# Linear attention with MoE: the store of a finished x behind the spread of quotients, a fifth buffer of numerators, the reciprocal behind the last decoding step

## The chip, the cores and the metric

One NeuronCore of a Trainium2 chip runs the kernel. The metric is the device time of one execution in microseconds (us). The kernel before takes 1066.59 us, the median of three runs (1066.25 to 1066.69).

## The reference

Attention without a softmax over the keys, for 8 batches, 8 heads, 576 positions and 64 values a head, and then a two-layer MLP on its result:

```python
def phi(x):
    proj = np.einsum('bhsd,df->bhsf', x, w_phi)
    proj = proj - np.max(np.abs(proj), axis=-1, keepdims=True)
    return np.concatenate([np.exp(proj), np.exp(-proj)], axis=-1)
q_p, k_p = (phi(q), phi(k))
kv = np.einsum('bhsf,bhsd->bhfd', k_p, v)
z = np.sum(k_p, axis=2)
num = np.einsum('bhsf,bhfd->bhsd', q_p, kv)
den = np.einsum('bhsf,bhf->bhs', q_p, z)[..., None] + 1e-06
x = num / den
...
h = x @ w_in
g = h - np.tanh(h)
return (g @ w_out).astype(np.float32)
```

The numerator `num` is divided by the denominator `den`; the quotient x is what the MLP reads.

## The kernel before

The program has two stages. In the first, attention goes through 32 units, a unit being two heads of one batch. In the second, the MLP multiplies the finished x by the weights. Both weight matrices arrive as 64-bit numbers and are decoded to float32 on the way, one tile of 128 x 512 in each period of the first stage.

`period(i)` (L644 to L703) is one pass of the first stage, for i from 3 to 31; `ramp` stands before it and `drain` behind it. The order of the work is written out by hand: the program sets a manual schedule, and each engine runs its instructions in the order in which the calls stand in `period`. A period works on six units at once, `a, c, p, r, q, o`, which are the units i, i-1, i-2, i-3, i-4 and i-5. What a unit goes through, with the names that the steps below use:

- **Unit a, the projection and its centring.** PE projects q and k (`project`, L327) into three places in PSUM: `pj`, `pa` and `pt`. DVE takes the largest absolute value of each (`m`, L345) and subtracts it (`t`, L346), in the order pj, pt, pa (`centre`). `pa` shares its PSUM bank with the numerators `po`: one buffer for both.
- **Unit c.** Its exponentials are taken, and `kv` multiplies keys by values (`pc`, L393, which reads the tile `v`).
- **Unit p.** `num` computes the numerators on PE (`po`, L442), and `num_copy` (L464 to L469) copies them by ACT into `d`, a tile of 128 x 576. The tile has four buffers: one in the pool `p1` for each fourth unit (tag `d0`), three in the pool `tail` for the rest and for the last three units (tag `d`).
- **Unit r.** `denom` computes the denominators on PE, `denom_copy` (L473) puts them into `dd`, and `den_recip_load` (L478) has SP's queue lay them out over 128 partitions as `dn`. At the end of the period `den_recip` (L483) takes the reciprocals `rn` on DVE, and `den_store` (L488) writes them to `rr` in DRAM.
- **Unit q.** `den_spread` (L493) reads `rr` back in two DMAs and spreads it as `rb`, a single buffer.
- **Unit o.** `den_mul` (L496) multiplies `d` by `rb` on POOL, and `x_store` (L499) writes the product, the finished x, to `xs` in DRAM.

A weight tile is decoded in five steps (`dec_0` on ACT, L279; `dec_1`, `dec_2` and `dec_3` on DVE, L283, L284, L287 and L291). They use the PSUM bank `pt` as scratch, behind its centring. On DVE the end of a period reads: L283, L284, L287, the reciprocal L483, then L291.

DMAs start from two queues. SP's queue takes, in the order of a period, `xs`, `dn`, `rb` twice, `v` (`load_v`, L307), up to two stores of prepared weights (`wd`, L112) and `rr`. ACT's queue takes the raw weights (L267, L272) and `qk` (L303). SP runs its DMA instructions one after the other, and an instruction that waits holds those behind it.

In `drain`, behind the last period, the last five units are finished while the second stage starts. The copies of units 30 and 31 stand there (L469), and the stores of units 27 and 28 (L499).

Of the kernel before, what the change touches and what calls it, by code (L numbers as in the profile page):

```python
# [9 lines left out]
F32 = mybir.dt.float32  # L10
# [10 lines left out]
P = 128  # L21
# [12 lines left out]
def tile_linear_attention_moe(  # L34
# [11 lines left out]
    B, H, S, D = dims  # L46
# [180 lines left out]
    with ExitStack() as c1:  # L227
        c0 = ExitStack()
        pq = c0.enter_context(tc.tile_pool(name="pq", bufs=2, side="right"))
        c1.enter_context(tc.tile_pool(name="padp", bufs=1)).tile([P, 8], F32, name="padp")  # L230
        p1 = c1.enter_context(tc.tile_pool(name="p1", bufs=1))
# [54 lines left out]
        def dec_2(u):  # L286
            nc.vector.scalar_tensor_tensor(u.a, u.lo, 29, u.a, ALU.logical_shift_right, ALU.bitwise_or)  # L287

        def dec_3(u):
            w = wpool.tile([P, DM], F32, tag="w", name=f"w{u.nm}")  # L290
            nc.vector.scalar_tensor_tensor(  # L291
                w.bitcast(U32), u.hi, 0x80000000, u.a, ALU.bitwise_and, ALU.bitwise_or
            )
            u.d[u.f] = w
# [5 lines left out]
        def load(u, queue=nc.sync):  # L300
            u.qk = pq.tile([P, PC], F32, tag="qk", name=f"qk{u.i}")
            for o, w in ((0, PC),) if u.i else ((5 * P, PC), (0, 5 * P)):
                queue.dma_start(u.qk[:, o:w], qkT[u.i][:, o:w])  # L303
# [6 lines left out]
        def project(u, parts):  # L310
            for part in parts:
                if u.t is None:
                    u.t = [pq.tile([P, 2, 5, F], F32, tag="t0", name=f"t{u.i}_0"), None]
                    u.m = [p2.tile([P, 2, 5], F32, tag="m0", name=f"m{u.i}_0"), p2.tile([P, 2, 4], F32, tag="m1", name=f"m{u.i}_1")]
                if part == "j":
                    u.pj = ps_pj.tile([P, 2, 512], F32, tag="pj", name=f"pj{u.i}")
                    bank, tiles = u.pj, range(4)
                elif part == "t":
                    u.pt = ps_t.tile([P, 2, 512], F32, tag="pt", name=f"pt{u.i}")
                    bank, tiles = u.pt, range(4, 5)  # L320
                else:
                    u.pa = ps_d.tile([P, 2, 512], F32, tag="po", name=f"pa{u.i}")
                    bank, tiles = u.pa, range(5, 9)
                for k, a in enumerate(tiles):
                    for e in range(2):
                        hs = slice(e * D, (e + 1) * D)
                        nc.tensor.matmul(  # L327
                            bank[:, e, k * F : (k + 1) * F], u.qk[hs, a * P : (a + 1) * P], wph[hs, :], start=True, stop=True
                        )
# [10 lines left out]
        def centre(u, parts, h=None):  # L340
            for part in parts:
                x, m, t = part_of(u, part)
                if h is not None:
                    x, m, t = x[:, :, h], m[:, :, h], t[:, :, h]
                nc.vector.tensor_reduce(m, x, AX.X, ALU.max, apply_absolute_value=True)  # L345
                nc.vector.tensor_tensor(t, x, m.unsqueeze(3).broadcast_to(list(t.shape)), ALU.subtract)  # L346
# [54 lines left out]
        def kadd(u):  # L401
            x = p2.tile([P, 2, 2, F], F32, tag="ss", name=f"ss{u.i}")
            nc.gpsimd.tensor_tensor(x, u.kp[:, :, 1], u.kp[:, :, 2], ALU.add)
            nc.gpsimd.tensor_tensor(x, x, u.kp[:, :, 3], ALU.add)
            nc.gpsimd.tensor_tensor(x, x, u.kp[:, :, 4], ALU.add)
            nc.gpsimd.tensor_tensor(x, x, u.kp[:, :, 0], ALU.add)
            u.ss = x
# [14 lines left out]
        def ksum_turn(u):  # L422
            nc.tensor.transpose(u.pu[:, 0:F], u.kst, ident)
# [38 lines left out]
                        )  # L462

        def num_copy(u):  # L464
            if u.i % 4 or u.i >= NU - 3:
                u.d = tail.tile([P, S], F32, tag="d", name=f"d{u.i}", bufs=3)
            else:
                u.d = p1.tile([P, S], F32, tag="d0", name=f"d{u.i}")
            nc.scalar.copy(u.d.rearrange("p (c n) -> p c n", c=2), u.po[:, :, 0:CH])  # L469

        def denom_copy(u):
# [18 lines left out]
        def den_spread(u):  # L490
            u.rb = tail.tile([P, S], F32, tag="rb", name=f"rb{u.i}", bufs=1)
            for e in range(2):
                nc.sync.dma_start(u.rb[e * D : (e + 1) * D, :], u.rr[e : e + 1, :].broadcast_to([D, S]))  # L493

        def den_mul(u, pin=lambda ins: ins):
            pin(nc.gpsimd.tensor_tensor(u.d, u.d, u.rb, ALU.mult))  # L496

        def x_store(u):
            nc.sync.dma_start(xs[u.b // 2][u.hp, :, (u.b % 2) * S : (u.b % 2 + 1) * S], u.d)  # L499

        units = []
        for i in range(B * NHP):
            u = Unit()
# [3 lines left out]
        NU = len(units)  # L507
# [9 lines left out]
        def unit(i):  # L517
            return units[i] if 0 <= i < NU else None

        def bank():  # L520
            return ps_c.tile([P, 512], F32, tag="pu", name="pu")
# [40 lines left out]
        for n, k in enumerate(order[:EARLY_K]):  # L562
            p = Prep(k, nc.gpsimd, early_tile, early_stage).steps()
            o = 5 + 7 * (n // 2) + 3 * (n % 2)
# [24 lines left out]
        def aside_at(i, late):  # L589
            for f in aside[i][late]:  # L590
                f()
# [57 lines left out]
        def period(i):  # L649
            a, c, p, r, q, o = (unit(i - n) for n in range(6))  # L650
            w = dec[i - 3]
            if i < NU - 1:
                aside_at(i, False)
            if o:
                den_mul(o)
                x_store(o)
            project(a, "jat")
            centre(a, "jt")
            kadd(c)
            aside_at(i, True)  # L660
            dec.append(dec_load(i - 2, nc.scalar))
            if i + 2 < NU:
                load(units[i + 2], nc.scalar)
            pu = bank()
            if r:
                denom(r, pu)
            ksum(p, pu)
            if r:
                denom_copy(r)
                den_recip_load(r)  # L670
            if q:
                den_spread(q)
            if i > 3:
                load_v(a)
            aside_at(i, 2)
            aside_at(i, 3)
            ksum_copy(p)
            kv_turn(p)
            kv_turn_copy(p)
            dec_0(w, a.pt)  # L680
            q_turn(c)
            ksum_turn(p)
            q_turn_rest(c, pu)
            q_exp(c)
            q_exp_rest(c)
            ksum_turn_copy(p)
            centre(a, "a")
            k_exp(a, 0)
            kv(c)
            kv_copy(c)  # L690
            k_exp(a, 1, (0,))
            dec_1(w)
            dec_2(w)
            if r:
                den_recip(r)
                den_store(r)
            dec_3(w)
            if i == NU - 1:
                x0_split(0)
            num(p)  # L700
            num_copy(p)
            if i < NU - 1:
                k_exp(a, 1, (1,))  # L703
# [98 lines left out]
        for i in range(3, NU):  # L802
            period(i)
# [487 lines left out]
```

## Time and profile before

| what | value |
|---|---|
| time, median of three runs | 1066.59 us |
| time of the profiled execution | 1067.74 us |
| its span | 1065.7 us |
| PE busy | 1052.3 us (99%) |
| DVE busy | 877.4 us (82%) |
| ACT busy | 781.4 us (73%) |
| POOL busy | 274.6 us (26%), nearly all of it in the first 310 us |
| PE on the chain that ended last | 89% |

The span lies between the first and the last instruction of the profiled execution. What its own time has beyond the span, 2.0 us, lies around it. A busy share is a mean over both stages; the first stage, about the first 315 us, has its own balance of engines and nearly all of the DMA traffic that the change touches. The granted clock of TensorE is the full one (1.00) in every stretch that was read.

### The profile page before, as it was taken

Reading aid. Unit: us, or ns where it says so; the run is one execution under the profiler, and the core shown is the slowest. Engines: PE = TensorE matmul, PEld = TensorE weight load, DVE = VectorE, ACT = ScalarE, POOL = GpSimd, SP = SyncE. Lnnn points to the kernel's source line nnn. Section 1 sums busy time; section 2 is a strip of 40 time slices with the busy share of each in tenths; the row PEclk is TensorE's granted clock in tenths of the full one; section 3 lists DMA queues with packets and bytes.
Section 4 is the critical chain, followed back from the end, with each engine's and each line's share of the span. In section 5 each row is a group of like instructions: output and inputs, shape, how many; then the busy total and the mean of one; then the engine's idle time right before and its main releaser. Section 6 shows DMA issues by size and latency. Waiting matters only on the chain.

```text
span 1065.7 us, 18843 instructions
## 1 busy us (share of the span) xinstructions
PE 1052.3 (99%) x7244; PEld 885.8 (83%) x7244; DVE 877.4 (82%) x1110; ACT 781.4 (73%) x1252; POOL 274.6 (26%) x235
## 2 busy tenths in 40 slices
PE   8999999999999999999999999999999999999998
PEld 6667666776658989999999999999999999999997
DVE  7999889999988988877887688877878778876776
ACT  5888788887888777776777676766677766776665
POOL 4798889898990000000000000000000000000000
PEclk9999999999999999999999999999999999999999
DMA  5688898999856463355444533355334543353311
GB/s 179 190 234 265 259 279 266 279 271 257 248 176 227 155 205 132 122 199 181 130 137 164 184 120 119 109 182 194 116 112 135 196 138 132 120 178 109 120 50 59
DMA packets 75593, 184.56 MB, mean 173 GB/s; under 512 B 15728, under 2 KB 30448, under 8 KB 75504
## 3 DMA queue, kind: packets, MB, share of 16 engines
q1 hardware_dynamic: 61104, 150.99, 43.0%
q10 hardware_dynamic: 14400, 32.38, 10.9%
q8 instruction: 57, 0.93, 0.4%
q14 instruction: 32, 0.26, 0.1%
HBM read 149.49 MB, written 33.70 MB: 172 GB/s over the span
## 4 chain that ended last, share of the span: by engine, by line
PE 89%; DVE 4%; POOL 2%; DMA 2%; ACT 1%; issue 1%; SPq 0%; DVEq 0%; POOLq 0%; ACTq 0%
PE A L142 18%; PE B L142 13%; PE po L946 12%; PE po L947 12%; PE po L952 12%; PE pc L393 6%; PE po L442 5%; PE pj L327 3%; PE pu L456 3%; PE pa L327 2%; PE ptt L357 2%; DMA dn<-dd 1%; PE pc L431 1%; PE pt L327 1%; POOL d L496 1%
## 5 line engine op out<-in xcount | busy, mean ns | idle before, releaser
L142 PE MATMUL A<-xo,wr 128*128 128x384 f32 x1152 | 231.9, 337 | 2.2 <-ACT u L870 2.2
L142 PEld LDWEIGHTS A<-xo,wr 128*128 128x128 f32 x1152 | 204.7, 188 | 14.6 <-ACT u L870 3.3
L142 PE MATMUL B<-xo,wr 128*128 128x384 f32 x864 | 174.1, 337 | 2.7 <-DVE xo L553 1.3
L870 ACT COPY u<-A 128x384 f32<-128x384 f32 x144 | 68.9, 479 | 140.3 <-PE A L142 139.9
L142 PEld LDWEIGHTS B<-xo,wr 128*128 128x128 f32 x864 | 152.4, 188 | 7.5 <-DVE xo L553 1.6
L946 PE MATMUL po<-who,ghx 128*128 128x512 f32 x288 | 112.3, 390 | 0.0
L946 PE MATMUL po<-who,ghy 128*128 128x512 f32 x288 | 112.3, 390 | 0.0
L947 PE MATMUL po<-wlo,ghy 128*128 128x512 f32 x288 | 112.1, 389 | 0.0
L947 PE MATMUL po<-wlo,ghx 128*128 128x512 f32 x288 | 112.1, 389 | 0.0
L496 POOL TENSOR_TENSOR d<-d,rb 128x576 f32<-128x576 f32 x32 | 46.6, 1457 | 203.3 <-DMA rb<-rr 171.4
L909 DVE SCALAR_TENSOR_TENSOR s2y<-s2y,thy 128x768 f32<-128x768 f32 x48 | 46.1, 960 | 57.1 <-ACT thy L900 57.1
L382 ACT ACTIVATE kp<-t 64x256 f32<-64x256 f32 (+1 forms) x126 | 88.4, 726 | 2.5 <-DVE t L346 1.0
L952 PE MATMUL po<-who,glx 128*128 128x512 f32 x288 | 80.9, 389 | 0.0
L894 ACT ACTIVATE yx<-hx 128x768 f32<-128x768 f32 (+1 forms) x49 | 41.0, 836 | 53.3 <-DVE hx L877 53.3
L952 PE MATMUL po<-who,gly 128*128 128x512 f32 x282 | 79.2, 389 | 0.0
L393 PE MATMUL pc<-kp,v 128*64 128x256 f32 x640 | 76.1, 384 | 0.0
L442 PE MATMUL po<-qe,kv 128*64 128x288 f32 x512 | 68.1, 408 | 0.0
L952 PEld LDWEIGHTS po<-who,glx 128*128 128x128 f32 x288 | 54.0, 188 | 11.2
L906 DVE SCALAR_TENSOR_TENSOR s2x<-s2x,yx 128x768 f32<-128x768 f32 (+1 forms) x49 | 46.2, 942 | 20.6 <-ACT s2x L895 19.2
L393 PEld LDWEIGHTS pc<-kp,v 128*64 128x64 f32 x640 | 43.1, 136 | 23.8 <-issue 4.5
L952 PEld LDWEIGHTS po<-who,gly 128*128 128x128 f32 x282 | 52.8, 188 | 11.1 <-DVE gly L924 0.2
L946 PEld LDWEIGHTS po<-who,ghx 128*128 128x128 f32 x288 | 54.1, 188 | 8.1 <-DVE hy L881 0.4
(174 smaller groups left out, 2262.0 us busy)
## 6 DMA issues: line engine op xcount, KB each, us to landing
wr<-wd SPq DMA_DIRECT2D x92, 512.0 KB, 3.5
wr<-wd SPq DMA_DIRECT2D x46, 768.0 KB, 4.3
qk<-in_qkT ACTq DMA_DIRECT2D x27, 576.0 KB, 6.9
v<-in_v SPq DMA_DIRECT2D x32, 320.0 KB, 5.3
rb<-rr SPq DMA_DIRECT2D x64, 144.0 KB, 4.7
xs<-d SPq DMA_DIRECT2D x32, 288.0 KB, 5.9
out<-o SPq DMA_DIRECT2D x35, 256.0 KB, 2.1
rawo<-in_moe_w_out ACTq DMA_DIRECT2D x16, 512.0 KB, 5.8
```

The costliest lines, as they stand in the source:

```text
L142: nc.tensor.matmul(bank[:, 0:HT], w[:, a, n, cs], x[:, b, c, :], start=start and i == 0, stop=i == 5, skip_group_check=not start,)
L327: nc.tensor.matmul(bank[:, e, k * F : (k + 1) * F], u.qk[hs, a * P : (a + 1) * P], wph[hs, :], start=True, stop=True)
L382: nc.scalar.activation(u.kp[h, :, j, s, :], u.t[r][h, :, x, :], AF.Exp, scale=1.0 - 2.0 * s)
L393: nc.tensor.matmul(u.pc[e * D : (e + 1) * D, 0 : 2 * F], u.v[:, j, e, :], u.kp[:, e, j, :, :], start=(j == first), stop=(j == last))
L442: nc.tensor.matmul(u.po[e * D : (e + 1) * D, c, 0:CH], u.kv[:, s, e * D : (e + 1) * D], u.qe[:, e, s, c * CH : (c + 1) * CH], start=(s == ...
L496: pin(nc.gpsimd.tensor_tensor(u.d, u.d, u.rb, ALU.mult))
L870: nc.scalar.copy(t, A[q][:, 0:HT])
L906: nc.vector.scalar_tensor_tensor(z.s[:, s], z.s[:, s], GC, z.y[:, s], ALU.add, ALU.mult)
L909: nc.vector.scalar_tensor_tensor(z.s[:, s], z.s[:, s], GK, z.th[:, s], ALU.mult, ALU.mult)
L946: nc.tensor.matmul(po, z.gh[:, ts], wh, start=first, stop=False)
L947: nc.tensor.matmul(po, z.gh[:, ts], wl, start=False, stop=False)
L952: nc.tensor.matmul(po, z.gl[:, ts], wh, start=False, stop=last)
```

## The change

It makes three edits, all in the first stage.

```diff
         def num_copy(u):
-            if u.i % 4 or u.i >= NU - 3:
+            if u.i >= NU - 3 or u.i % 5 > 1:
                 u.d = tail.tile([P, S], F32, tag="d", name=f"d{u.i}", bufs=3)
+            elif u.i % 5 or u.i >= NU - 6:
+                u.d = p1.tile([P, S], F32, tag="d0", name=f"d{u.i}")
             else:
-                u.d = p1.tile([P, S], F32, tag="d0", name=f"d{u.i}")
+                u.d = pq.tile([P, S], F32, tag="d1", name=f"d{u.i}", bufs=1)
...
             if o:
                 den_mul(o)
-                x_store(o)
...
             if q:
                 den_spread(q)
+            if o:
+                x_store(o)
...
             dec_1(w)
             dec_2(w)
+            dec_3(w)
             if r:
                 den_recip(r)
                 den_store(r)
-            dec_3(w)
```

`pq` is the pool on the right side of SBUF that holds `qk`, `v` and `t`. With the fifth buffer, unit u shares its buffer with unit u+5 where it was u+4, except for the last units: unit 30 takes the buffer of unit 27 (before: of unit 26), and unit 31 that of unit 28 (before: of unit 27).

The first place is SP's queue in period 14 (`rr10` is the reciprocals of unit 10 on their way to DRAM, `d9` the product of unit 9). Before:

```order
L488 DMA rr10_1828<-rn10_1826 128x9 [waits DMAHW7_49,DVE_49]
L499 DMA xs1_89<-d9_1575 128x576 [waits DMAHW0_49,Pool_49]
L478 DMA dn11_1903<-dd11_1901 128x1x9 [waits DMAHW3_49,Activation_49]
L493 DMA rb10_1905<-rr10_1828 64x576 [waits DMAHW7_49,DMAHW4_49,DMAHW2_49]
L493 DMA rb10_1905<-rr10_1828 64x576 [waits DMAHW5_49]
L307 DMA v14_1908<-in_v5 128x640 [waits DMAHW6_49,PE_49]
L112 DMA wd3_0_101<-wr3_0_1446 128x512
```

After:

```order
L490 DMA rr10_1830<-rn10_1828 128x9 [waits DMAHW7_49,DVE_49]
L480 DMA dn11_1902<-dd11_1900 128x1x9 [waits DMAHW2_49,Activation_49]
L495 DMA rb10_1904<-rr10_1830 64x576 [waits DMAHW3_49,DMAHW7_49,DMAHW1_49,Pool_49]
L495 DMA rb10_1904<-rr10_1830 64x576 [waits DMAHW4_49]
L501 DMA xs1_89<-d9_1575 128x576 [waits DMAHW5_49]
L307 DMA v14_1908<-in_v5 128x640 [waits DMAHW6_49,PE_49]
L112 DMA wd3_0_101<-wr3_0_1446 128x512
```

The store `xs` moved behind the load `dn` and both spreads `rb`, and the wait for POOL's product went from the store to the first spread.

The second place is DVE at the end of period 17. Before:

```order
L283 TENSOR_SCALAR pt17_2271<-pt17_2271 128x512 [waits Activation_49]
L284 TENSOR_SCALAR pt17_2271<-pt17_2271 128x512 [waits DVE_49]
L287 SCALAR_TENSOR_TENSOR pt17_2271<-rawo4_2151,pt17_2271 128x512 [waits DMAHW5_49,DVE_49]
L483 RECIPROCAL rn14_2360<-dn14_2304 128x9 [waits DMAHW3_49,DMAHW0_49]
L291 SCALAR_TENSOR_TENSOR wo4_2364<-rawo4_2151,pt17_2271 128x512 [waits DVE_49]
L345 TENSOR_REDUCE m18_0_2384<-pj18_2386 128x2x4 [waits PE_49]
```

After:

```order
L283 TENSOR_SCALAR pt17_2270<-pt17_2270 128x512 [waits Activation_49]
L284 TENSOR_SCALAR pt17_2270<-pt17_2270 128x512 [waits DVE_49]
L287 SCALAR_TENSOR_TENSOR pt17_2270<-rawo4_2150,pt17_2270 128x512 [waits DMAHW4_49,DVE_49]
L291 SCALAR_TENSOR_TENSOR wo4_2360<-rawo4_2150,pt17_2270 128x512 [waits DVE_49]
L485 RECIPROCAL rn14_2362<-dn14_2303 128x9 [waits DMAHW7_49,DMAHW3_49]
L345 TENSOR_REDUCE m18_0_2383<-pj18_2385 128x2x4 [waits PE_49]
```

The reciprocal and its wait for the DMA moved behind the last decoding step; behind it comes, as before that step did, the first centring of the next unit.

The third place is ACT in `drain`, where unit 30's numerators are copied. Before:

```order
L427 COPY ks30_4307<-pu_4237 128x128 [waits PE_49,Activation_49]
L377 ACTIVATE qe31_4304<-pu_4237 128x2x64 x2
L399 COPY kvt31_4322<-pc31_4311 128x256 [waits PE_49,Activation_49]
L469 COPY d30_4349<-po30_4332 128x576 [waits DMAHW1_49,PE_49,Pool_49]
L279 ACTIVATE pt_4351<-rawo14_4266 128x512 [waits DMAHW3_49,DVE_49]
```

After:

```order
L427 COPY ks30_4307<-pu_4237 128x128 [waits PE_49,Activation_49]
L377 ACTIVATE qe31_4304<-pu_4237 128x2x64 x2
L399 COPY kvt31_4322<-pc31_4311 128x256 [waits PE_49,Activation_49]
L471 COPY d30_4349<-po30_4332 128x576 [waits DMAHW0_49,PE_49,Pool_49]
L279 ACTIVATE pt_4351<-rawo14_4266 128x512 [waits DMAHW3_49,DVE_49]
```

The order stayed, but the copy now waits on another DMA's semaphore: the store of unit 27 in place of that of unit 26.

## Rows read from the trace of the kernel before

**Rows 1.** Windows: a stretch, its length, busy us of each engine, PEclk, DMA share, GB/s

```profile
30.00:300.00 270.00, 268.44 (x3086) 185.42 (x3086) 244.96 (x342) 220.17 (x429) 238.72 (x201) 1.00 0.86 252
...
98.00:134.00 36.00, 34.82 (x408) 24.12 (x405) 30.95 (x46) 27.96 (x54) 30.43 (x27) 1.00 0.89 254
```

**Rows 2.** Timeline, a plain period, DVE: start us, us, instruction, [idle before <-releaser]

```profile
163.92 1.23 DVE L346 TENSOR_TENSOR t<-pa,m 128x1024 f32<-128x1024 f32 x1
...
166.52 0.70 DVE L287 SCALAR_TENSOR_TENSOR pt<-rawo,pt 128x512 uint32<-128x512 uint32 x1
167.13 0.21 DVE L483 RECIPROCAL rn<-dn 128x9 f32<-128x9 f32 x1
167.25 0.69 DVE L291 SCALAR_TENSOR_TENSOR wo<-rawo,pt 128x512 uint32<-128x512 uint32 x1
168.50 1.23 DVE L345 TENSOR_REDUCE m<-pj 128x8 f32<-128x1024 f32 x1 [0.56 <-PE pj L327]
```

**Rows 3.** Timeline, the same plain period, PE

```profile
165.25 2.12 PE L442 MATMUL po<-qe,kv 128*64 128x288 f32 x16
167.29 1.16 PE L327 MATMUL pj<-wph,qk 64*128 64x128 f32 x16
```

**Rows 4.** Timeline, the period with the longest wait, DVE

```profile
115.00 1.23 DVE L346 TENSOR_TENSOR t<-pa,m 128x1024 f32<-128x1024 f32 x1
...
120.20 0.22 DVE L483 RECIPROCAL rn<-dn 128x9 f32<-128x9 f32 x1 [1.91 <-DMA dn<-dd]
...
120.88 1.22 DVE L345 TENSOR_REDUCE m<-pj 128x8 f32<-128x1024 f32 x1
```

**Rows 5.** Timeline, that period and the next, PE

```profile
118.37 1.16 PE L327 MATMUL pj<-wph,qk 64*128 64x128 f32 x16
...
121.02 0.49 PE L327 MATMUL pt<-wph,qk 64*128 64x128 f32 x4 [0.58 <-DVE wi L291]
...
124.82 2.38 PE L393 MATMUL pc<-kp,v 128*64 128x256 f32 x20
```

**Rows 6.** Timeline, DVE, the other reciprocals that waited over 0.60 us

```profile
99.58 0.22 DVE L483 RECIPROCAL rn<-dn 128x9 f32<-128x9 f32 x1 [0.66 <-DMA dn<-dd]
109.48 0.22 DVE L483 RECIPROCAL rn<-dn 128x9 f32<-128x9 f32 x1 [1.10 <-DMA v<-in_v]
148.99 0.22 DVE L483 RECIPROCAL rn<-dn 128x9 f32<-128x9 f32 x1 [0.98 <-DMA dn<-dd]
262.41 0.22 DVE L483 RECIPROCAL rn<-dn 128x9 f32<-128x9 f32 x1 [0.88 <-DMA dn<-dd]
```

**Rows 7.** Timeline, SP's queue in the period with the longest wait

```profile
111.95 0.32 SPq L499 DMA_DIRECT2D xs<-d  x1
112.72 0.59 SPq L478 DMA_DIRECT2D dn<-dd  x1
...
114.78 0.59 SPq L307 DMA_DIRECT2D v<-in_v  x1
```

**Rows 8.** DMA issues, whole run: count, KB each, median us from issue to landing

```profile
v<-in_v SPq DMA_DIRECT2D x32, 320.0 KB, 5.3
...
xs<-d SPq DMA_DIRECT2D x32, 288.0 KB, 5.9
...
rr<-rn SPq DMA_DIRECT2D x32, 4.5 KB, 3.3
```

**Rows 9.** Timeline of `drain`: SP, DVE, ACT; last, the view of tile xs

```profile
303.04 0.32 SPq L499 DMA_DIRECT2D xs<-d  x1
303.46 0.59 SPq L478 DMA_DIRECT2D dn<-dd  x1
...
305.92 0.21 DVE L483 RECIPROCAL rn<-dn 128x9 f32<-128x9 f32 x1 [0.40 <-DMA dn<-dd]
...
306.95 0.64 ACT L469 COPY d<-po 128x576 f32<-128x576 f32 x1 [1.01 <-issue]
...
DMA to landing us min/median/max: 2.1/5.9/8.0
```

## The prediction

> **What bounds the kernel now.** I read the view by stretches first. In the first stage PE is busy 268.4 of 270 us, DVE 245.0 and POOL 238.7 [rows 1], at the full granted clock, and DMA moves 252 GB/s with its engines at a share of 0.86. So PE has next to no time to give, and what can be won is a wait that stretches a period. The change touches no PE work and nothing in the second stage except by starting it earlier.
>
> The timeline of one plain period shows what sets its length. DVE ends the centring of `pa` at 165.15 (163.92 + 1.23) [rows 2]. This frees the bank in which PE then writes `po`, from 165.25, and behind it PE projects `pj` from 167.29 to 168.45 [rows 3]. DVE begins the next unit's centring at 168.50, after an idle time of 0.56 us that `pj` ended [rows 2]. From the end of `t<-pa` to `m<-pj` it is 3.35 us, and the rest of the loop is DVE's own centring up to the next `t<-pa`. So the loop runs through DVE (centring) and PE (`po`, `pj`), and the decoding and the reciprocal lie beside the PE part, with 0.56 us to spare. The reader is to see that a reciprocal that waits up to 0.56 us costs nothing, and that each tenth beyond it lengthens the period.
>
> The view of DVE's reciprocals gives what goes beyond. The longest wait is 1.91 us, for `dn` [rows 4]; four more are over 0.60 us: 0.66, 1.10, 0.98 and 0.88 [rows 6]. The second of these is put down to another transfer, `v`; since the reciprocal reads `dn` alone, I take that label for a landing at the same time. The shorter ones cost next to nothing. Less 0.56 each, the five are 1.35, 0.10, 0.54, 0.42 and 0.32, together 2.73 us. The longest can be checked: `t<-pa` ends at 116.23 and `m<-pj` starts at 120.88 [rows 4], 4.65 us in place of 3.35, so 1.30 and not 1.35. With 0.05 us off each, **the late reciprocals cost 2.5 us** of the profiled execution. In the worst period the late decoding step also held PE's projection into `pt` for 0.58 us [rows 5]; that lies inside the 1.30.
>
> **The change part by part.** No instruction is added or removed; all three edits move or rename.
>
> *The last decoding step ahead of the reciprocal.* In a plain period DVE ends L287 at 167.22, and the reciprocal takes 0.21 us [rows 2]. If only the reciprocal is left to come, it may start as late as 168.45 - 0.21 = 168.24 before the next centring is late, so its wait may last 1.0 us in place of 0.56. The decoding step fills it, and frees `pt` for PE. Alone this would bring the waits of 0.66, 0.88 and 0.98 to nothing, leave about 0.1 of the one of 1.10 and about 0.85 of the longest (`pj` ends at 119.53 [rows 5], the reciprocal at 120.42 [rows 4]). It gains 2.5 - 0.9 = 1.6 us. In a plain period it starts `rr` some 0.6 us later. The spread behind `rr` waits for a landing that takes 3.3 us [rows 8], and may be 0.6 us later at the worst; it gains more than that by the next edit, since the store no longer runs ahead of it.
>
> *The store behind the spread.* Before, 288 KB of `xs` [rows 8] went to SP's queue 0.77 us ahead of `dn` [rows 7], so `dn` had to be moved behind them. `dn` took from 112.72 [rows 7] to the reciprocal at 120.20 [rows 4], 7.5 us for 4.5 KB; that is a queue, not a transfer. How much earlier it lands no row shows. The lower bound is nothing, if other transfers hold it. The upper bound is the 5.9 us from a store's issue to its landing [rows 8]. At the 254 GB/s of that stretch [rows 1], 288 KB take 1.16 us, an estimate; I take this one, as it is what the queue does with these bytes. It is more than the 0.85 us that the first edit leaves, so the worst period is repaired too. A gain below nothing has no place: behind the change fewer bytes stand ahead of `dn`, and POOL's product no longer does.
>
> What now stands behind the spread pays: the store starts about 2.5 us later, and `v` by one SP issue, 0.32 us [rows 7], and what lies around it, say 0.4. `v` issued at 114.78 [rows 7] lands after 5.3 us [rows 8] at 120.1, and the multiplication that reads it starts at 124.82 [rows 5], so 4 us of cover stand behind a loss of 0.4. The spread now waits itself for POOL's product; that product is done before the store's issue at 111.95 [rows 7], while the spread comes after `dn`. It costs nothing; were POOL 1 us later, `v` and the weight stores would be.
>
> The Trainium skill, in "DMA: Bandwidth & Descriptors", section "Queues, rings and completion order", speaks against taking the whole 1.16 us: the count that reports a DMA is a strongly ordered write, which lands only after every earlier write of that engine, across its queues. By that, `dn` still waits for the loads that ACT's queue issued before it, and the sum would be that of the first rival, 1.6 us. No row here tells the two queues' shares of the delay apart.
>
> *The fifth buffer.* The copy of unit u+4 came more than a period behind the store that it had to wait for. The longest landing is 8.0 us [rows 9], and a period is longer, as two reciprocals in a row at 99.58 and 109.48 show [rows 6]. The buffer hides nothing and costs nothing in the body. It only matters in `drain`, below.
>
> **The sum.** Of the 2.5 us I leave 0.2 for a `dn` that still comes late, as DMA stays as busy as before: 2.3 us gained. Against the profiled execution's own time that is 1067.74 - 2.3 = 1065.4 us (its span 1065.7, 2.0 us around it). That execution lies 1.15 us above the median; if this is a constant of profiling, the median goes to 1066.59 - 2.3 = **1064.3 us**, 0.22% less. A change of 0.2% (2.1 us) is about what a measurement of this kernel can tell from none, so the forecast stands just over it.
>
> **Rivals.**
>
> 1. *`dn` does not land earlier*, because the transfers of ACT's queue hold it, and only the exchange on DVE acts. For it speaks the DMA share of 0.89 [rows 1]; against it the 288 KB just ahead on the same queue. Gain 1.6: 1065.0 us.
> 2. *The waits are smaller without the profiler.* The runs differ by 0.4 us, and the profiled one lies 1.15 us above their median. If all of that were late reciprocals, the others lose only 2.5 - 1.15 = 1.35 us: 1065.2 us.
> 3. *Nothing comes of it*: another transfer takes the place of the late one, or the time returns in the second stage. No row points to it. 1066.6 us.
> 4. *A new wait in `drain` makes it slower.* Unit 30's numerators now go to the buffer of unit 27, whose store is issued at 303.04, and the copy is at 306.95 [rows 9]. If the landing takes more than 3.9 us, ACT waits, and PE's next numerators wait behind it for the bank. At the longest landing of 8.0 us the copy is 4.1 us late, and the net is 4.1 - 2.5 = 1.6 us slower: 1068.2 us. It passes the old time from a landing of 6.4 us, and 0.2% from 8.5. For it speaks the median of 5.9. Against it: `dn`, issued 0.42 us behind that store on the same queue, had released the reciprocal at 305.92 [rows 9], so the store has landed, or nearly so, 1 us before the copy.
>
> **How the numbers follow.** Forecast 0.46, rival 1 0.17, rival 2 0.23, rival 3 0.07, rival 4 0.07. The forecast gives the chance of faster, 0.46. Rivals 1 to 3 lie within 0.2%, and so do two parts in seven of the last: 0.49. Slower is left with 0.05. Of the range, the low end is 1063.6: the whole 2.5 us, and 0.5 us for what the late periods set off behind them (loads and stores that were issued later in turn). The high end is 1066.4, 0.2 us under the old median, which takes in rivals 1 and 2 with something to spare. Outside stay rivals 3 and 4 and a little on the low side.
>
> **What would show it.** In the changed profile `dn` should be issued as before, and a reciprocal that waits should begin at least 0.8 us sooner behind that issue than 7.5 us in the worst period. Idle time ahead of `m<-pj`, ended by `pj`, should stand in every period, the time from `t<-pa` to `m<-pj` should be 3.35 us throughout, and PE's wait in `pt` for the decoding step should be gone. Unit 30's copy should not start later against `po` than now. The prediction is wrong if reciprocals still run into the next centring, if ACT or PE idle in `drain` behind that copy, or if the first stage ends 2 us sooner while the total does not.

## The result and the profile after

| what | before | changed |
|---|---|---|
| median of five runs | 1066.48 us | 1079.73 us |
| lowest and highest | 1065.85, 1066.69 | 1076.66, 1082.91 |
| profiled execution, its span | 1067.74, 1065.7 | 1081.09, 1079.1 |

The change makes the kernel 1.2% slower: the ratio of the times is 1.0119 [1.0103, 1.0135]. The forecast was 1064.3 us, and even the range ended at 1066.4.

The page of the changed profile, the engines, the chain that ended last and one of the costliest groups; last, the same group on the page of before:

```profile
PE 1056.2 (98%) x7244; PEld 891.5 (83%) x7244; DVE 880.1 (82%) x1110; ACT 781.5 (72%) x1252; POOL 273.9 (25%) x235
...
PE 84%; DMA 6%; DVE 4%; POOL 3%; ACT 1%; issue 1%; SPq 1%; DVEq 0%; POOLq 0%; ACTq 0%
...
L393 PE MATMUL pc<-kp,v 128*64 128x256 f32 x640 | 79.9, 398 | 11.0 <-DMA v<-in_v 9.0
...
L393 PE MATMUL pc<-kp,v 128*64 128x256 f32 x640 | 76.1, 384 | 0.0
```

The chain was 89% PE before, and 2% DMA; now DMA has 6% of it. The idle time in the third row is new: PE idles 11.0 us ahead of the matmuls that read `v`. The waits between 30 and 330 us say the same, first of all engines, then of SP's queue. The columns are engine, line, what it waited for, us in total, times, longest:

```profile
DVE m L345 <- PE pj L327: 26.2, 27, 4.4
...
PE pc L393 <- DMA v<-in_v: 9.0, 5, 2.5
...
DVE rn L485 <- DMA dn<-dd: 2.7, 5, 1.0
```

```profile
SPq L495 <- DMA rr<-rn: 52.5, 21, 6.4
```

The wait that the change was to shorten is short: the reciprocal (L485) waits for `dn` in five periods, 1.0 us at the longest, where it was 1.91 [rows 4]. What is new stands on SP: the spread (L495) waits for `rr` 52.5 us in 21 periods, and behind it wait the store, `v`, the weight stores and the next `rr`. SP's list of waits before the change has no wait of the spread for `rr`.

The windows over two stretches and over one bad period (stretch, its length, busy us of PE, PEld, DVE, ACT, POOL, then PEclk, DMA share, GB/s) show when it happens:

```profile
30.00:170.00 140.00, 140.00 (x1623) 97.29 (x1619) 129.44 (x180) 115.15 (x226) 120.48 (x103) 1.00 0.81 247
170.00:300.00 130.00, 118.98 (x1319) 84.97 (x1320) 109.20 (x150) 96.53 (x188) 107.67 (x91) 0.96 0.74 238
...
191.00:194.00 3.00, 0.94 (x10) 0.73 (x9) 2.90 (x5) 2.94 (x6) 2.84 (x3) 1.00 0.99 355
...
196.00:198.00 2.00, 2.00 (x12) 1.36 (x10) 0.73 (x2) 0.73 (x2) 1.83 (x2) 0.50 0.05 21
```

Up to 170 us PE never idles, which is what the change was to bring; before, it was busy 268.44 of 270 us [rows 1]. Behind 170 us six periods get long. The timeline of DVE, a good period and two bad ones:

```profile
165.41 0.21 DVE L485 RECIPROCAL rn<-dn 128x9 f32<-128x9 f32 x1
166.06 1.23 DVE L345 TENSOR_REDUCE m<-pj 128x8 f32<-128x1024 f32 x1 [0.44 <-PE pj L327]
...
187.75 1.23 DVE L345 TENSOR_REDUCE m<-pj 128x8 f32<-128x1024 f32 x1 [2.84 <-PE pj L327]
...
304.90 1.23 DVE L345 TENSOR_REDUCE m<-pj 128x8 f32<-128x1024 f32 x1 [4.40 <-PE pj L327]
```

From one first `m<-pj` to the next it is 9.42 us in a plain period. Six periods, which end at 175.93, 187.75, 200.99, 212.03, 225.41 and 304.90, take 9.87, 11.82, 13.24, 11.04, 13.38 and 13.38 us. That is 16.2 us beyond six times 9.42. PE's timeline has the reason:

```profile
170.47 2.38 PE L393 MATMUL pc<-kp,v 128*64 128x256 f32 x20 [0.38 <-DMA v<-in_v]
...
182.29 2.38 PE L393 MATMUL pc<-kp,v 128*64 128x256 f32 x20 [2.34 <-DMA v<-in_v]
...
193.84 3.31 PE L393 MATMUL pc<-kp,v 128*64 128x256 f32 x20 [2.06 <-DVE t L346]
...
298.01 3.81 PE L393 MATMUL pc<-kp,v 128*64 128x256 f32 x20 [2.46 <-DMA v<-in_v]
```

The idle time ahead of these matmuls is 11.0 us in sum, the row of the page. One of the six waits is put down to `t` and not to `v`. There `t` ended at 193.82 us, and the last update that reports the landing of `v` came at 193.71, 0.13 us ahead of the matmuls; in the period before, it came as far ahead of them (182.16, then 182.29). So this wait too may be one for `v`; its label doesn't decide it. The other 5.2 us go to TensorE's clock: after the wait of 2.06 us the granted clock was at 0.50, the level of 1.2 GHz, between 196 and 198 us (last row of the windows), and the same 20 matmuls took 3.31 us and not 2.38; two more of these groups took over 3.8. The granted clock of 0.96 over the 130 us behind 170 us (second row of the windows) gives the same 5.2 us, an estimate. So 16.2 us are lost, and 2.5 us of late reciprocals [rows 4, 6] are gone: 13.7 us slower by the periods, against 13.35 between the two profiled executions (1081.09 - 1067.74). Behind the first stage nothing changed: from the last `m<-pj` to the end of the span it is 774.2 us, and was 774.3.

**How `v` came late.** SP's queue in a good period and in the bad stretch:

```profile
103.00 0.59 SPq L480 DMA_DIRECT2D dn<-dd  x1
103.70 1.11 SPq L495 DMA_DIRECT2D rb<-rr  x2
...
109.02 0.32 SPq L490 DMA_DIRECT2D rr<-rn  x1
...
113.12 1.10 SPq L495 DMA_DIRECT2D rb<-rr  x2
...
169.05 0.59 SPq L480 DMA_DIRECT2D dn<-dd  x1
172.93 1.10 SPq L495 DMA_DIRECT2D rb<-rr  x2
174.08 0.58 SPq L501 DMA_DIRECT2D xs<-d  x1
174.76 0.38 SPq L307 DMA_DIRECT2D v<-in_v  x1
175.18 0.50 SPq L112 DMA_DIRECT2D wd<-wr  x1
175.77 0.43 SPq L490 DMA_DIRECT2D rr<-rn  x1
178.92 0.59 SPq L480 DMA_DIRECT2D dn<-dd  x1
185.11 1.10 SPq L495 DMA_DIRECT2D rb<-rr  x2
...
190.74 0.60 SPq L480 DMA_DIRECT2D dn<-dd  x1
197.87 1.10 SPq L495 DMA_DIRECT2D rb<-rr  x2
```

At 103 us the spread followed `dn` within 0.11 us. At 172.93 it starts 3.3 us behind the end of `dn`'s issue (172.93 - 169.64), one period on 5.6 us, then 6.5. From the issue of `rr` to the spread that waits for it, it was 4.10 us at 109, and in the periods that follow 4.8, 4.5, 5.4, 5.75, 6.4, 7.1, 9.3 and 9.8: from the third on, each late spread is followed by a later one, until PE's stalls give the queue time again. The chain of the same stretch has the two transfers that carry the lateness:

```profile
174.76 7.40 DMA v<-in_v
...
182.29 2.38 PE pc L393 x20
...
201.52 8.18 DMA rr<-rn
```

`v` landed after 5.3 us before [rows 8] and takes 7.40 here. When the packets moved tells why (grouped by queue and packet size, in a good and a bad period of the changed kernel; the sizes belong to these tiles alone):

```
                        good period          bad period
SP   rb, xs  2304 B     104.99 - 107.99      174.19 - 176.91
SP   v       2560 B     106.93 - 109.71      176.42 - 181.72
SP   wd      4096 B     108.31 - 110.96      179.05 - 183.65
SP   rr        36 B     109.87 - 111.02      180.90 - 184.59 (with dn)
ACT  raw    512 KB      110.10 - 114.21      177.54 - 181.87
ACT  qk      576 KB     112.11 - 116.16      180.96 - 184.55
```

In the good period SP's transfers are nearly through when ACT's loads begin: the weight store and `rr` still run for 0.9 us beside them. The ACT rows are 512 KB of raw weights and 576 KB of `qk`. In the bad period the burst starts 5.14 us behind the issue of `dn` in place of 1.99, and meets them: `v` takes 5.3 us on the engines where it took 2.8, and `rr`, issued at 175.77 right behind `v` and `wd`, lets the spread go at 185.11 only. In the good period its packets were through 2.0 us after its issue at 109.02. The Trainium skill, in "DMA: Bandwidth & Descriptors", section "Queues, rings and completion order", says that an engine takes one queue's descriptors in ring order and goes round between the queues that have work. The packets agree: `rb` and `xs`, `v`, `wd`, `rr` begin in the order of their issue, and ACT's packets run between them.

`drain` shows nothing. Unit 30's copy starts at 320.42 after an idle time of 1.02 us; before it was 1.01 [rows 9].

### The profile page after: what moved, and what is told of

It reads as the page before. It is cut to its first block, busy times and chain, and to the rows that moved or that the text cites. A ratio compares the mean times of both kernels' runs of the same rounds, so it can differ in the third digit from the quotient of the medians.

```text
span 1079.1 us, 18821 instructions
## 1 busy us (share of the span) xinstructions
PE 1056.2 (98%) x7244; PEld 891.5 (83%) x7244; DVE 880.1 (82%) x1110; ACT 781.5 (72%) x1252; POOL 273.9 (25%) x235
## 4 chain that ended last, share of the span: by engine, by line
PE 84%; DMA 6%; DVE 4%; POOL 3%; ACT 1%; issue 1%; SPq 1%; DVEq 0%; POOLq 0%; ACTq 0%
PE A L142 17%; PE B L142 13%; PE po L949 12%; PE po L950 12%; PE po L955 11%; PE pc L393 5%; PE po L442 4%; DMA v<-in_v 2%; PE pj L327 2%; DMA rr<-rn 2%; PE pu L456 2%; PE pa L327 2%; PE ptt L357 1%; DMA rb<-rr 1%; POOL d L498 1%
## 5 line engine op out<-in xcount | busy, mean ns | idle before, releaser
L393 PE MATMUL pc<-kp,v 128*64 128x256 f32 x640 | 79.9, 398 | 11.0 <-DMA v<-in_v 9.0
L393 PEld LDWEIGHTS pc<-kp,v 128*64 128x64 f32 x640 | 46.3, 141 | 35.1 <-DVE t L346 9.9
L345 DVE TENSOR_REDUCE m<-pj 128x8 f32<-128x1024 f32 x32 | 39.2, 1224 | 27.3 <-PE pj L327 27.3
```

Source lines behind the costliest of these rows:

```text
L393: nc.tensor.matmul(u.pc[e * D : (e + 1) * D, 0 : 2 * F], u.v[:, j, e, :], u.kp[:, e, j, :, :], start=(j == first), stop=(j == last))
```

## The experiments

The times of before beside them are 1066.54 us (31 runs), 1066.50 (18) and 1066.88 (19) for the three groups below; single runs of it went from 1065.09 to 1070.61. Each edit is shown against the changed kernel where nothing else is said.

### First group: which edit is it

**One: the store goes back ahead of `dn`.** The later reciprocal and the fifth buffer stay.

```diff
             if o:
                 den_mul(o)
+                x_store(o)
...
-            if o:
-                x_store(o)
```

> The change with its store of x put back ahead of dn; fifth buffer and late reciprocal stay. Theory 1 (the store's new place, between the spread rb and the store of reciprocals rr on SP's queue, puts 288 KB and one more issue ahead of rr; the next spread waits for rr's landing and holds all that SP issues behind it): the slowdown is gone, 1064.9 to 1066.5 us, rr lands within 4 us of its issue, PE does not wait for v. Theory 2 (the reciprocal 0.6 us later makes rr and so the spread late): it stays near 1079 us. Theory 3 (DMA has no capacity left, and the late reciprocals were what held the kernel back): still slower than before, 1068 us or more, as the reciprocals no longer wait over 1 us.

Measured: 1066.49 us (1065.58 to 1069.93, ten runs), ratio 1.0003 [0.9993, 1.0012]. So the later reciprocal alone costs nothing and gains nothing. SP's waits show that its spread is late too, but less:

```profile
SPq L495 <- DMA rr<-rn: 16.5, 16, 2.3
```

No period of the profiled execution is longer than 9.58 us. A spread that is up to 2.3 us late is harmless by itself; the lateness has to feed on something.

**Two: the reciprocal goes back ahead of `dec_3`.** The moved store and the fifth buffer stay.

```diff
             dec_2(w)
-            dec_3(w)
             if r:
                 den_recip(r)
                 den_store(r)
+            dec_3(w)
```

> The change with the reciprocal put back ahead of the last decoding step; fifth buffer and the store behind the spread stay. Theory 1: stays slow, 1074 to 1083 us, SP's spread still waits for rr for over 30 us in all. Theory 2: back to 1066 us or below. Theory 3: as slow as the change, 1075 us or more, since the store alone already lets dn land early.

Measured: 1065.89 us (1064.96 to 1074.10, ten runs), ratio 1.0003 [0.9984, 1.0022]. The median is at the old time, but two of the ten runs are at 1070.91 and 1074.10, above every run of before. In the profiled execution, the fastest of the ten, the spread waits for `rr` 4.3 us in nine periods, 0.9 us at most. The moved store alone costs nothing in most runs, but seems to stand close to an edge; neither of those two runs was profiled. The first theory had this kernel at 1074 to 1083 us, and the second had experiment one near 1079. Neither edit by itself does it.

**Three: the fifth buffer alone.** Both moves are undone.

```diff
             if o:
                 den_mul(o)
+                x_store(o)
...
-            if o:
-                x_store(o)
...
             dec_2(w)
-            dec_3(w)
             if r:
                 den_recip(r)
                 den_store(r)
+            dec_3(w)
```

> The fifth buffer alone. Theories 1 to 3: no difference, 1066.0 to 1067.0 us. Theory 4 (the buffer in the right pool shifts addresses and puts waits on landings into the copies and the second stage's first tiles): near 1079 us.

Measured: 1066.89 us (1065.46 to 1067.94), ratio 0.9998 [0.9988, 1.0007]. The buffer is innocent. This kernel issues its first stage in the order of before, and its profile has something else to tell. One of the waits, all engines:

```profile
DVE rn L485 <- DMA dn<-dd: 2.0, 5, 0.7
```

The same wait had single rows of 1.91, 1.10, 0.98 and 0.88 us before [rows 4, 6]. This execution, of 1065.46 us, is the fastest of its kernel, 1.4 us under its median; the one profiled before was 1.15 above its own. From the fourth `m<-pj` to the last it is 264.34 us here and was 266.85 there: the 2.5 us of late reciprocals are gone without either move. How much of them the usual execution has isn't shown. The profiled executions of experiments one and four have the same 264.3 us and yet took 1066.01 and 1066.32, with their first `m<-pj` at 9.60 us, where it is at 9.05 here. So executions differ outside the loop as well, where the moves don't reach.

**Four: the store moves on, behind the issue of `rr`.** The later reciprocal stays.

```diff
-            if o:
-                x_store(o)
...
             if r:
                 den_recip(r)
                 den_store(r)
+            if o:
+                x_store(o)
```

> The change with the store of x moved further, behind the store of reciprocals rr at the end of the period; fifth buffer and late reciprocal stay. Neither dn nor rr then has the store just ahead of it. Theory 1: 1064.0 to 1065.5 us, no reciprocal waits over 0.6 us, rr lands within 4 us, v on time. Theory 2 or 3: slow, 1070 us or more.

Measured: 1066.64 us (1065.44 to 1067.59), ratio 0.9999 [0.9989, 1.0009]. The spread waits for `rr` 15.0 us in 14 periods, 1.9 at most, and nothing follows from it: from the spread's issue to that of `v` it is 1.20 us again, where the change made it 1.83. So it matters whether the store stands on SP between the spread and the next `rr`. The 1064.0 to 1065.5 us that were expected did not come, although the reciprocals hardly wait (0.7 us, once).

### Second group: what the store does in its new place

The change itself ran again beside these.

> The change as it is, once more, beside the next three. Theory 5 (both edits together: the late reciprocal leaves rr 4.1 in place of 4.8 us until the spread is due, and the store ahead of v and the weight stores makes rr land later once the spread is late, so that the lateness feeds itself): 1074 to 1084 us, the spread late by more from period to period until PE waits for v. Theory 6 (the slow runs of the change were a state of that chip alone): 1066 us.

Measured: 1076.61 us (1073.47 to 1085.36, four runs), ratio 1.0105 [1.0042, 1.0168]. PE waits for `v` 10.9 us in seven periods, and SP's spread for `rr` 42.3 us in 17, so the profile read above was no exception.

**Five: the spread goes behind `v` and the weight stores**, so that it holds nothing back when it waits.

```diff
-            if q:
-                den_spread(q)
             if o:
                 x_store(o)
             if i > 3:
                 load_v(a)
             aside_at(i, 2)
             aside_at(i, 3)
+            if q:
+                den_spread(q)
```

> The change with the spread moved behind the store of x, v and the weight stores, so that a late rr holds none of these; reciprocal late, as in the change, and the same bytes ahead of rr but for the spread's own. Theory 5: the feedback is cut; 1065 to 1067 us, no wait of PE for v. Theory 7 (it is the bytes ahead of rr that count, whatever the spread holds): slow, over 1070 us.

Measured: 1070.23 us (1068.35 to 1073.81, nine runs), ratio 1.0036 [1.0023, 1.0049]. The waits of the profiled execution, first SP, then the other engines:

```profile
SPq L495 <- DMA rr<-rn: 0.5, 1, 0.5
```

```profile
POOL d L498 <- DMA rb<-rr: 21.2, 16, 3.7
...
ACT wr L185 <- POOL s L168: 8.5, 6, 2.0
```

The growth is gone: the spread no longer waits, and PE has no wait for `v`. What is left of the loss seems to be another one: the quotients themselves are spread late, POOL waits for them up to 3.7 us (before up to 2.5), and ACT for POOL. Three periods are 0.6 to 1.0 us too long, and about 2 us more are lost behind the last period. So this does not win, but about two thirds of the loss go with the waiting in front of `v` and `rr`. The edit does two things, though: the spread holds nothing back, and it comes later itself, 5.3 to 7.9 us behind the issue of `rr` in place of 4.1, so `rr` has more time to land.

**Six: the store back, and a store of 4.5 KB in its new place** (`spare` is a DRAM tile that nobody reads). This tells the place from the bytes.

```diff
             if o:
                 den_mul(o)
+                x_store(o)
...
             if o:
-                x_store(o)
+                nc.sync.dma_start(spare, q.rn)
```

> The change with the store of x back ahead of dn, and in its new place a DMA of 4.5 KB into a spare tensor (work that the change does not have). It keeps the extra issue on SP between the spread and v, 0.6 us, and takes the 288 KB away. Theory 7 and 5, if the bytes make rr late: as without the store there, 1066 to 1067 us. If the 0.6 us of issue on SP are what lengthens the loop: over 1070 us.

Measured: 1072.60 us (1070.46 to 1079.27, five runs), ratio 1.0046 [1.0029, 1.0063]. SP's waits, and those of PE:

```profile
SPq L495 <- DMA rr<-rn: 45.4, 20, 6.1
```

```profile
PE pc L393 <- DMA v<-in_v: 7.3, 6, 2.6
```

With 1/64 of the bytes the same growth sets in, from 1.78 us between spread and `v`. The profiled execution is the slowest of the five, 1079.27. The kernel has one DMA more in each period than the change, so it isn't a pure test of the bytes, but it shows that the 288 KB aren't needed in this place: 0.6 us of issue time and 4.5 KB are enough.

**Seven: the weight stores of that place go behind `rr`.**

```diff
-            aside_at(i, 2)
             aside_at(i, 3)
...
             if r:
                 den_recip(r)
                 den_store(r)
+            aside_at(i, 2)
```

> The change with the stores of prepared weights (256 to 512 KB in most periods) moved behind the store of reciprocals rr; store of x and reciprocal as in the change. Theory 5 and 7: rr has fewer bytes ahead of it, lands in 4 us or less, the spread is on time: 1065 to 1067 us. Theory 8 (the place of the store itself, or the order in which DMAs share their eight semaphores, makes it slow): near 1080 us.

Measured: 1069.93 us (1066.21 to 1073.54, ten runs), ratio 1.0029 [1.0012, 1.0045]. The profiled execution is the best of them, 1066.21, with waits for `rr` of 2.2 us at most. About two thirds of the loss are gone, and from run to run it goes either way. With the weight stores out of the stretch between spread and `rr`, a late spread does less, but not nothing.

### Third group: the collision, and a better place

**Eight: ACT's loads (raw weights and `qk`) are issued behind `dn`**, away from SP's burst.

```diff
-            dec.append(dec_load(i - 2, nc.scalar))
-            if i + 2 < NU:
-                load(units[i + 2], nc.scalar)
...
                 den_recip_load(r)
+            dec.append(dec_load(i - 2, nc.scalar))
+            if i + 2 < NU:
+                load(units[i + 2], nc.scalar)
```

> The change with ACT's two loads of a period (raw weights 512 KB, qk 576 KB) issued some 3 us later, behind the copy of the denominators and the issue of dn. Theory 9 (the late reciprocal moves the issue of rr from 5.3 to 6.0 us behind that of dn; ACT's next loads come at 7.1; a late rr falls behind their 1.1 MB on the DMA engines, and the SP issues between the spread and v push it there): with the loads out of its way rr lands in 4 us, the spread is on time, 1065 to 1066.5 us. Theory 5 without the loads (SP's own loop alone): still slow, over 1070 us. Dn, now ahead of these loads, should land 2 us or more sooner than before in either case, shown by no wait of the reciprocal.

Measured: 1077.62 us (1077.50 to 1079.63, four runs), ratio 1.0102 [1.0080, 1.0125]. As slow as the change, but for another reason:

```profile
SPq L495 <- DMA rr<-rn: 5.3, 10, 0.9
```

```profile
PEld pu L423 <- ACT kst L420: 11.8, 26, 0.7
```

The waits for `rr` fall from 52.5 us to 5.3, as they should if the growth needs ACT's loads beside SP's burst. But now nearly every period takes 9.7 to 10.1 us, because the two issues stand on ACT ahead of the copy `kst`, for which PE's weight loads wait in 26 periods. A longer period also gives `rr` about 0.5 us more to land. The edit mixes these effects; its time says nothing on the first.

**Nine: the same move of ACT's loads in the kernel before.** It was to show whether these loads hold `dn`, as the prediction's first rival had it.

> The kernel before with ACT's two loads issued behind dn, nothing else. If the delay of dn came from ACT's 1.1 MB ahead of it (as the rule of completion order had it), no reciprocal waits and the runs lie at 1065.3 to 1066 us; if it came from the store of x on SP's queue, reciprocals wait as before, 1066 to 1067 us.

Measured: 1084.08 us (1082.66 to 1085.23, four runs), ratio 1.0157 [1.0129, 1.0184].

```profile
DVE rn L483 <- DMA dn<-dd: 19.1, 16, 2.9
```

`dn` came later and not earlier, as the loads now start at the same moment as `dn`. A miss as a test: it doesn't tell whether a completion has to wait for the other queue's writes, which is the rule on strongly ordered counts that the prediction quoted. That stays open.

**Ten: experiment six with the reciprocal ahead of `dec_3`.**

```diff
             if o:
                 den_mul(o)
+                x_store(o)
...
             if o:
-                x_store(o)
+                nc.sync.dma_start(spare, q.rn)
...
             dec_2(w)
-            dec_3(w)
             if r:
                 den_recip(r)
                 den_store(r)
+            dec_3(w)
```

> The kernel with the small DMA between spread and v (store of x ahead of dn), with the reciprocal put back ahead of the last decoding step. Theory 5 and 9: the spread has its 4.8 us back; mostly 1066 to 1067 us, with now and then a slow run, as with the store there. If the extra issue on SP alone made it slow: 1070 us or more, as with the late reciprocal.

Measured: 1071.33 us (1066.24 to 1077.90 in nine runs, a tenth at 1085.58), ratio 1.0032 [1.0009, 1.0055]. The earlier reciprocal brings the waits for `rr` from 45.4 us down to 15.3, and the best run to 1066.24, but not the time back. A DMA more on SP is a cost even with the old margin.

**Eleven: the store behind `rr`, the reciprocal ahead of `dec_3`.**

```diff
-            if o:
-                x_store(o)
...
             dec_2(w)
-            dec_3(w)
             if r:
                 den_recip(r)
                 den_store(r)
+            if o:
+                x_store(o)
+            dec_3(w)
```

> The store of x behind the store of reciprocals, the reciprocal ahead of the last decoding step as before, fifth buffer. Neither dn nor rr has the store ahead of it and rr keeps its 4.8 us. Theory 5 and 9: 1065.3 to 1066.3 us, every run under 1068, the spread never waits for rr by over 1 us. It would be the fastest if the reciprocals' waits of some executions of the kernel before are what its runs lose.

Measured: **1065.69 us** (1065.17 to 1065.92, ten runs), ratio 0.9983 [0.9972, 0.9994]. It is faster than both kernels, 0.2% below the one before, and its ten runs lie within 0.75 us where those of before go over 5. SP's timeline, one period:

```profile
165.26 0.32 SPq L490 DMA_DIRECT2D rr<-rn  x1
165.63 1.37 SPq L501 DMA_DIRECT2D xs<-d  x1
169.39 0.60 SPq L480 DMA_DIRECT2D dn<-dd  x1
170.09 1.10 SPq L495 DMA_DIRECT2D rb<-rr  x2
171.28 0.54 SPq L307 DMA_DIRECT2D v<-in_v  x1
```

and its windows, to be read beside [rows 1]:

```profile
30.00:300.00 270.00, 270.00 (x3117) 187.09 (x3113) 246.93 (x344) 222.56 (x433) 241.46 (x202) 1.00 0.84 253
```

The spread follows `dn` within 0.3 us in every period, `v` comes 1.19 us behind it here, the store has the empty stretch between `rr` and `dn`, and PE never idles. The gain over before is 1.2 us by the medians. Where it comes from isn't shown: PE is busy 270.00 of these 270 us in the profiled executions of experiments one, three and four too, and the medians of those kernels are at the old time.

## Why the prediction was wrong

**The loop and the late reciprocals: right in kind, wrong in size.** With the change the reciprocal waits 1.0 us at most, `t<-pa` to `m<-pj` is 3.35 us in every period up to 170 us, and PE's wait in `pt` for the decoding step is gone. That part of the change does what was said. But the 2.5 us were summed from one execution, 1.15 us above the median, and taken off the median. They were there, in that execution: experiment three, in the same order, loses nothing to them in its fastest one. The second rival saw that ("the others lose only 2.5 - 1.15 = 1.35 us", so 1065.2), and the best version, at 1065.69 with runs from 1065.17, comes nearest to it. Its size isn't shown: experiments one and four hold the late reciprocals down too, and their medians are 1066.49 and 1066.64. It isn't shown to be the profiler either: executions differ, outside the loop too.

**The step that failed: `rr`'s slack.** The prediction said that the spread behind `rr` "may be 0.6 us later at the worst; it gains more than that by the next edit, since the store no longer runs ahead of it". The delay was sized well: the reciprocal starts 5.78 us behind `dn`'s issue and not 5.05, so 0.73 us. What was wrong is "at the worst". That sentence compares one landing of 3.3 us [rows 8] with one window. The window was 4.83 us from the issue of `rr` to the moment the spread is due, and became 4.10; the landing, which is itself a matter of what stands ahead, let the spread wait in 21 periods. Nor did the next edit make up for it: with the store moved and the reciprocal in its old place, in experiment two, the spread waits for `rr` in nine periods, and before the change in none.

The window alone doesn't do it. The kernel before had shorter ones in its periods with a late reciprocal, down to 3.44 us (263.06 to 266.50), and up to 300 us its spread never began more than 0.12 us behind the end of `dn`'s issue. What the 0.73 us also changed is the order against ACT's raw weights. A period of before, with a late reciprocal, and one of the change:

```profile
109.73 0.32 SPq L488 DMA_DIRECT2D rr<-rn  x1
110.33 0.39 ACTq L267 DMA_DIRECT2D rawi<-in_moe_w_in  x1
...
108.95 0.41 ACTq L267 DMA_DIRECT2D rawi<-in_moe_w_in  x1
109.02 0.32 SPq L490 DMA_DIRECT2D rr<-rn  x1
```

Before, `rr` was issued ahead of these 512 KB in every period, by 0.1 us or more, even where the whole loop was late. In the change it stands 0.07 us behind them as a rule, and further behind once the spread is late. It is so in experiments one and four as well, and their spread is up to 2.3 us late. In experiments two and eleven `rr` is ahead again, and the spread is 1.0 us late at the most. No run moves these loads and nothing else, so what this order costs by itself isn't measured.

And a late spread isn't paid once. It stands first in SP's queue, with the store, `v`, the weight stores and the next `rr` behind it. When it is late by more than an estimated 2.6 us, the next `rr` is issued late as well: `rr` is ready 6.02 us behind `dn`'s issue (5.78, the reciprocal's 0.21 and 0.03), SP comes to it 0.59 + lateness + 2.84 us (172.93 to 175.77) behind that issue. The edge is nearer where more weight stores stand in between. Below it the spread's lateness rises or falls from period to period: between 122 and 160 us it grew from 0.8 to 2.8 us, while `rr` was issued 0.4 us late at most, so that part of the growth lies in the landing. Above 2.6 us, in both traces of the change, it never comes down again before stalls of PE give the queue time to catch up. Then it begins again: the period that ends at 304.90 is the second such loss.

**The store behind the spread was taken as free but for 0.4 us of `v`.** "4 us of cover stand behind a loss of 0.4" counted the cover of `v` with the spread on time. The price of this edit isn't `v`'s delay, 0.6 us and not 0.4, but the room that it takes between spread and `rr`: without it the edge is an estimated 0.6 us farther, at 3.2 us, and the longest wait in experiment one is 2.3. With the reciprocal back, `rr` is ready 0.73 us sooner and the edge is at 1.9, but the longest wait of experiment two is 0.9. So either edit keeps the lateness under its edge in the profiled executions, and both together don't: the kernel doesn't lose the sum of two prices, of which each measured next to nothing, but passes a point from which the delay feeds itself. That it takes both to slow every run is shown by experiments one, two and four; with the moved store alone two runs of ten are over 1070 us. That the feedback runs through what the waiting spread holds is seen in SP's timeline, and experiment five fits, though it gives `rr` more time as well. That ACT's loads take part is seen in the packet times, and the waits of experiment eight fit; its time doesn't tell. How the growth divides between issue time on SP and sharing with ACT's loads stays open.

**The rivals.** The third named the kind of thing, "another transfer takes the place of the late one", and gave it no price. The fourth was no help: the new wait isn't in `drain`, where unit 30's copy waits as long as before. So a rival on the slower side was there, but in the wrong place. None asked what the spread holds when `rr` is late, though the rows for it were at hand: `rr` at 3.3 us [rows 8] and `dn` at 7.5 us for the same 4.5 KB when it stood in a queue. This told that such a landing may double.

**The fifth buffer** cost nothing and hid nothing, as said.

## What to carry to other kernels

In a queue that runs its DMAs in order, a round trip through DRAM (a store, then a load that waits for it) has a slack like any other loop: take the time from its store's issue to the due time of its load, compare it with the longest landing and not with the median, look which large transfers of other queues are issued just ahead of the store, and list everything that stands behind the waiting load, the next round's own store above all. If that store stands behind it, a delay isn't paid once but handed on. A bulk store belongs behind the small store that starts the round trip, and a gain that is a sum of small DMA waits should be seen in more than one execution before it is counted.

## What the runs showed of the hardware that was not expected

- A store of 4.5 KB, `rr`, landed after 3.3 us in the median of before [rows 8] and after more than 8 us (8.18 in the chain) where it was issued right behind `v` and a weight store while ACT's loads ran.
- A stall of 2.06 us ahead of `pc` was followed by a granted clock of 0.50 (196 to 198 us); one of 2.34 us, a period earlier, was not, as the 20 matmuls behind it took 2.38 us. In the stalled periods the clock cost about 5.2 us beside the 11.0 us of idling.
- A DMA's issue is part of its engine's order: two issues moved on ACT ahead of one small copy lengthened nearly every period, by 0.3 to 0.6 us (experiment eight).
